# Chunk attention and a cosine router on one core: v and k loads in exchanged queues, and another order of the steps in the attention loop

## The chip, the cores and the metric

The kernel runs on one core of one Trainium2 chip. The metric is the device time of one execution in microseconds; before the change the median of three runs is 674.3 us (673.04 to 680.07). Engines: PE (TensorE, its matmuls; PEld are its weight loads), DVE (VectorE), ACT (ScalarE), POOL (GpSimd) and SP (SyncE, which only issues transfers). Transfers are issued from SP's queue or from POOL's.

## What is computed

Attention within chunks of 64 tokens, over 8 batches, 8 heads, 576 tokens and 64 channels per head; its output, 4608 tokens of 512 channels, goes through a router that gives each token to one of 8 experts, and through that expert's two layers. All of it is in float32.

```python
# q, k, v: (8, 8, 576, 64); chunk = 64, nc = 9
scores = scale * np.matmul(q_c, k_c.transpose(0, 1, 2, 4, 3))
scores = scores - np.max(scores, axis=-1, keepdims=True)
attn = np.exp(scores)
attn = attn / (np.sum(attn, axis=-1, keepdims=True) + 1e-09)
out = np.matmul(attn, v_c)
...
x = np.ascontiguousarray(attn_out.transpose(0, 2, 1, 3)).reshape(B * S, H * D)
...
xn = x / (np.linalg.norm(x, axis=-1, keepdims=True) + 1e-06)
logits = xn @ en.T / tau
expert_idx = np.argmax(logits, axis=1)
...
    h = np.maximum(x[mask] @ w1[e], 0.0)        # w1[e]: 512 x 1024
    out[mask] = gate_w[mask, None] * (h @ w2[e])  # w2[e]: 1024 x 512
```

## The kernel before

The kernel has two stages. The first is a loop over `t` from -3 to 38 in steps of one tile of 128 tokens (two chunks, all heads); there are `NT` = 36 tiles, 4.5 per batch. It computes the attention output of each tile, its squared norm and its logits, finds a place for each of its tokens among rows grouped by expert, and writes the token's row (2304 bytes: 512 channels, logits, token number, squared norm) to that place in a DRAM tensor `spots`. The second stage reads groups of 64 rows per expert from `spots`, multiplies them with the expert's weights and writes the results to the tokens' rows of the output. It is nearly all matmuls, and the diff does not touch it.

The schedule is manual: each engine runs its instructions in the order in which the program text issues them, and each queue its transfers. An instruction that has to wait for a buffer or an operand holds everything behind it on its engine. The steps of the loop work on different tiles at the same time:

- `load_qk(t)` loads a tile of k and of q, 256 KB each, as 1024 pieces of 256 bytes; a tile that spans two batches takes two transfers of each. There are four buffers of each, so a buffer is free again when `turn_qk` of four tiles before has read it. `load_v(b)` loads a batch's v, 8 transfers of one head (64 rows with 9 pieces of 256 bytes), into one of two buffers.
- `turn_qk(t)` transposes k and q on PE (128x128 float32 against the identity, four each); ACT copies k's out of PSUM, DVE q's.
- `scores(t)` runs 32 matmuls of 64x64; DVE takes the row maxima and subtracts them. There is one PSUM buffer for the scores, so the next tile's matmuls wait for this subtraction. `weights(t)` is the exp, in place, on ACT.
- `turn_a(t)` transposes the exp on PE, and ACT copies it out. `values(t)` runs 32 matmuls of 64x64 with v and a column of ones; DVE adds 1e-9 to the sums (the tile `rs`), takes the reciprocal and multiplies (L662) into a row buffer `xr`, of which there are eight. An iota on POOL writes the token numbers into the same row.
- `turn_x(t)` transposes that output on PE; ACT copies it out and takes the squares. Its operand is what L662 wrote.
- Every four tiles `logits` runs 32 matmuls of 128x32, `copy_logits` turns and copies the result, `pick` chooses the expert on DVE, and `place`, one tile later, counts ranks on PE and DVE. `put` then sends one tile's rows per tile with an indirect transfer on POOL, which is the scatter to `spots`.
- `constants()` fills small tables on POOL and a blank row block, all in tile 0; `clear_first()` writes the blank rows to nine blocks of `spots` from SP in tile 1. `load_early` (from tile 26, on SP) reads the first groups back, and `load_first` loads the first experts' weights, 4 MB in tile 28 and 4 MB in tile 30, from SP. `early_parts` are matmuls of the second stage that are put between the last tiles.

The transposes share three PSUM buffers (tag `tr`), in the order in which they are issued. Before the change the queues are these: k's first four tiles on SP and the others on POOL, q on POOL, v on SP.

Of the kernel before, what the change touches and what calls it, by code (L numbers as in the profile page):

```python
# [11 lines left out]
I32 = mybir.dt.int32  # L12
AF = mybir.ActivationFunctionType
ALU = mybir.AluOpType
# [4 lines left out]
P = 128  # L19
CH = 64  # L20
ROUND = 12582912.0
NO_ROW = 200000
# [3 lines left out]
def kernel(  # L26
# [11 lines left out]
    nc = tc.nc  # L38
    B, H, S, Dh = q.shape
    E, D = moe_expert_emb.shape  # L40
# [5 lines left out]
    NT = N // P  # L46
    NCB = S // CH
    G = P // 2
# [5 lines left out]
    NE = 4  # L54
# [20 lines left out]
    W = D + 64  # L75
# [94 lines left out]
    def first_rows(s, j, n):  # L170
        r0 = (0, E - 1)[s] * R + G * j
        return spots[r0 : r0 + G * n, :]
# [273 lines left out]
    with (  # L446
# [59 lines left out]
        in_g = one.tile([P, 1], FP32, name="in_g")  # L506
        e_p = one.tile([P, 1], FP32, name="e_p")

        def constants():
            nc.gpsimd.iota(io_i, pattern=[[1, NST]], base=0, channel_multiplier=0)  # L510
            nc.gpsimd.iota(part_i, pattern=[[0, 1]], base=0, channel_multiplier=1)
            make_upper_triangular(nc, sltb, val=1.0, diag=False)
            nc.gpsimd.memset(onesb, 1.0)
            nc.gpsimd.memset(blank, 0.0)
            nc.gpsimd.memset(blank[:, D + TOK : D + TOK + 1].bitcast(I32), NO_ROW)
            nc.gpsimd.memset(ones, 1.0)
            nc.gpsimd.memset(before, 0.0)
            nc.gpsimd.memset(eqb_all[:, 0], 0.0)
            nc.gpsimd.memset(jump[:, 1], 1.0)
            nc.gpsimd.memset(nb[:, 0:1], float((SPARE + R) // G))  # L520
            nc.gpsimd.tensor_copy(io, io_i)
            nc.gpsimd.tensor_copy(at, part_i)
            nc.gpsimd.tensor_scalar(pref, io[:, 0:E], -1.0, float(E), ALU.mult, ALU.add)
            nc.gpsimd.tensor_scalar(e_base, io[:, 0:E], float(R), None, ALU.mult)
            nc.gpsimd.tensor_scalar(second, at, float(G), None, ALU.is_ge)
            nc.gpsimd.tensor_scalar(is_0, at, 2.0, None, ALU.is_lt)
            nc.gpsimd.tensor_scalar(lim, at, -float(P), float(G * NE), ALU.mult, ALU.add)
            nc.gpsimd.tensor_scalar(step, second, -2.0, 1.0, ALU.mult, ALU.add)
            nc.gpsimd.tensor_scalar(first_s, second, -1.0, 1.0, ALU.mult, ALU.add)
            nc.gpsimd.tensor_scalar(back, io, -1.0, float(NST - 1), ALU.mult, ALU.add)  # L530
            nc.gpsimd.tensor_scalar(more_g, back, float(LEAST - NE), None, ALU.is_ge)
            nc.gpsimd.tensor_scalar(pair_g, back, float(LEAST - NE), None, ALU.is_equal)
            nc.gpsimd.tensor_tensor(more_g, more_g, pair_g, ALU.add)
            nc.gpsimd.tensor_tensor(pair_g, back, more_g, ALU.subtract)
            nc.gpsimd.memset(more_e[:, NSW - 1 : NSW], 1)
            nc.gpsimd.tensor_scalar(e_0, second, float(E - 1), None, ALU.mult)
            nc.gpsimd.tensor_scalar(e_1, e_0, 1.0, None, ALU.add)
            nc.gpsimd.tensor_scalar(ends_e, io[:, 0:E], 0.0, None, ALU.is_equal)
            nc.gpsimd.tensor_scalar(full, io[:, 0:E], float(E - 1), None, ALU.is_equal)
            nc.gpsimd.tensor_tensor(ends_e, ends_e, full, ALU.add)  # L540
            nc.gpsimd.tensor_scalar(done, ends_e, float(NE), None, ALU.mult)
            nc.gpsimd.tensor_scalar(ends_e, ends_e, is_0, None, ALU.mult)
            nc.gpsimd.tensor_scalar(in_g, second, -float(G), at, ALU.mult, ALU.add)
            nc.gpsimd.tensor_scalar(e_p, second, float(R), None, ALU.mult)
            nc.gpsimd.tensor_scalar(
                base_h, io[:, 0 : E // 2], 2.0 * R, e_p, ALU.mult, ALU.add
            )

        def clear_first():

            for s in range(2):
                nc.sync.dma_start(
                    out=first_rows(s, 0, NE).rearrange("(j p) w -> p j w", p=G),
                    in_=blank[0:G].unsqueeze(1).to_broadcast([G, NE, W]),
                )
            nc.sync.dma_start(out=spots[SPARE : SPARE + G, :], in_=blank[0:G])

        before = one.tile([P, E], BF16, name="before")
        qk_t, qkT, v_t, st = {}, {}, {}, {}

        def load_qk(t):

            for src, nm, eng in (
                (k, "kx", nc.sync if t < 4 else nc.gpsimd),
                (q, "qx", nc.gpsimd),
            ):
                x = qk_p.tile([P, H, Dh], FP32, tag=nm, name=nm)
                done = 0
                while done < P:
                    b, s = divmod(t * P + done, S)  # L570
                    n = min(P - done, S - s)
                    eng.dma_start(  # L572
                        out=x[done : done + n],
                        in_=src[b, :, s : s + n, :].rearrange("h p d -> p h d"),
                    )
                    done += n
                qk_t[nm, t] = x.rearrange("p h d -> p (h d)")

        def load_v(b, c0=0, c1=NCB, eng=nc.sync):

            t = v_sb[b % 2]
            for h in range(H):
                r0 = CH * (h % 2)
# [58 lines left out]
        def values(t):  # L642
# [3 lines left out]
            for i in range(NPAIR):  # L646
# [18 lines left out]
                rs.unsqueeze(3).to_broadcast([P, 2, NPAIR, Dh]),  # L665
                ALU.mult,
            )
            nc.gpsimd.iota(
                xr[:, t % NX, D + TOK : D + TOK + 1].bitcast(I32),
                pattern=[[0, 1]],  # L670
                base=P * t,
                channel_multiplier=1,
            )
            st[t] = {"x": x}

        def turn_x(t):
# [344 lines left out]

        early_t = 26
        ends = {sum(sizes[: b + 1]) - 1: b for b in range(len(sizes))}
        for t in range(-3, NT + 3):
# [202 lines left out]
```

## Time and profile before

One execution was profiled. It took 673.1 us; its span, from the first to the last instruction, is 671.3 us, with a mean granted TensorE clock of 0.983.

| engine | busy us of the span | in 73.13 to 88.42, a stretch of four tiles |
|---|---|---|
| PE | 623.0 | 14.52 |
| PE weight loads | 346.2 | 12.42 |
| DVE | 421.3 | 13.44 |
| ACT | 443.8 | 11.07 |
| POOL | 155.3 | 11.62 |

Row after row, the profile names line, engine, operation and tiles: `sc` are the scores in PSUM, `mx` their maxima, `a` what the exp works on, `pv` the values in PSUM, `xr` the row buffers, `tr` the transposes in PSUM. A timeline row gives the start and duration in microseconds, then, in brackets, how long the engine stood idle before it and what ended this. "issue" is idle time for which the profile shows no cause. The slices of the page are 16.8 us each. Waits are listed as total, number of times and longest one.

### The profile page before, as it was taken

Reading aid. Unit: us, or ns where it says so; the run is one execution under the profiler, and the core shown is the slowest. Engines: PE = TensorE matmul, PEld = TensorE weight load, DVE = VectorE, ACT = ScalarE, POOL = GpSimd, SP = SyncE. Lnnn points to the kernel's source line nnn. Section 1 sums busy time; section 2 is a strip of 40 time slices with the busy share of each in tenths; the row PEclk is TensorE's granted clock in tenths of the full one; section 3 lists DMA queues with packets and bytes.
Section 4 is the critical chain, followed back from the end, with each engine's and each line's share of the span. In section 5 each row is a group of like instructions: output and inputs, shape, how many; then the busy total and the mean of one; then the engine's idle time right before and its main releaser. Section 6 shows DMA issues by size and latency. Waiting matters only on the chain. (4 is left out here: it accounts for less than half of the span.)

```text
span 671.3 us, 24844 instructions
## 1 busy us (share of the span) xinstructions
PE 623.0 (93%) x9744; PEld 346.2 (52%) x9744; DVE 421.3 (63%) x1140; ACT 443.8 (66%) x776; POOL 155.3 (23%) x237
## 2 busy tenths in 40 slices
PE   6869998998898989999999999999999999999993
PEld 5658787885443446666434444334444444444431
DVE  4738888986598536547675566757655666565430
ACT  5627776775225847777777867778777677877740
POOL 8827787843310100010000100010001000100101
PEclk9969999999999989999999999999999999999997
DMA  9978999989818711113786111777811115411111
GB/s 256 275 180 233 275 288 269 275 246 371 330 55 300 285 45 35 50 34 111 290 305 210 50 42 43 290 274 253 327 52 50 38 47 167 166 43 34 50 31 35
DMA packets 94590, 112.66 MB, mean 168 GB/s; under 512 B 52364, under 2 KB 72588, under 8 KB 94456
## 3 DMA queue, kind: packets, MB, share of 16 engines
q1 hardware_dynamic: 82728, 72.84, 34.1%
q0 software_dynamic: 11696, 38.04, 17.0%
q8 instruction: 81, 1.33, 0.8%
q14 instruction: 53, 0.43, 0.2%
q10 hardware_dynamic: 32, 0.02, 0.0%
HBM read 334.71 MB, written 22.69 MB: 532 GB/s over the span
## 5 line engine op out<-in xcount | busy, mean ns | idle before, releaser
L413 PE MATMUL y_ps<-w,hT 128*32 128x512 f32 (+1 forms) x2368 | 273.2, 589 | 3.1 <-DVEq L299 3.1
L361 ACT ACTIVATE h<-C 64x256 f32<-64x256 f32 x264 | 178.6, 676 | 95.5 <-DVE C L374 68.9
L413 PEld LDWEIGHTS y_ps<-w,hT 128*32 128x32 f32 x2368 | 93.2, 110 | 153.6 <-issue 123.8
L428 POOL DMA_INDIRECT out_dram<-y,spot x36 | 34.9, 968 | 437.0 <-ACT C L377 198.0
L374 DVE TENSOR_TENSOR C<-C,h 128x256 f32<-128x256 f32 x231 | 96.1, 416 | 49.2 <-DVEq L299 42.5
L342 PE MATMUL h<-w,S 128*32 128x256 f32 x1056 | 98.1, 379 | 1.8 <-DVE w L291 1.8
L342 PE MATMUL h<-sums,xbT 128*32 128x256 f32 x1056 | 97.0, 379 | 0.0
L342 PE MATMUL h<-w,xbT 128*32 128x256 f32 x1056 | 79.4, 380 | 7.0 <-ACTq L299 5.8
L368 DVE STREAM_TRANSPOSE hT<-h 128x512 f32<-128x512 f32 x66 | 46.7, 708 | 44.1 <-ACT h L361 44.0
L342 PEld LDWEIGHTS h<-w,xbT 128*32 128x32 f32 x1056 | 40.8, 110 | 43.2 <-ACTq L299 13.5
L342 PEld LDWEIGHTS h<-w,S 128*32 128x32 f32 x1056 | 49.2, 110 | 24.4 <-DVE w L291 1.5
L342 PEld LDWEIGHTS h<-sums,xbT 128*32 128x32 f32 x1056 | 48.9, 110 | 21.9 <-ACT C L377 0.4
L227 DVE TENSOR_SCALAR rn<-rn 128x1 f32<-128x1 f32 x37 | 5.7, 153 | 72.1 <-ACT rn L224 72.1
L342 PE MATMUL h<-sums,S 128*32 128x256 f32 x528 | 48.7, 379 | 0.0
L800 POOL DMA_INDIRECT spots<-xr,dest x36 | 37.1, 1029 | 35.0 <-DVE dest L765 10.1
L203 DVE STREAM_TRANSPOSE xbT<-xin 128x256 f32<-128x256 f32 x73 | 44.4, 646 | 0.5 <-DVE hT L368 0.5
L224 ACT ACT_TABLE_LOAD x34 | 43.6, 1283 | 0.9 <-issue 0.4
L421 ACT ACTIVATE y<-y_ps,gate 128x512 f32<-128x512 f32 (+1 forms) x37 | 25.2, 682 | 28.6 <-issue 14.7
L231 ACT ACT_TABLE_LOAD x34 | 43.6, 1283 | 0.6
L682 ACT COPY xT<-tr 128x512 f32<-128x512 f32 x36 | 21.1, 586 | 34.2 <-PE tr L680 34.2
L651 PE MATMUL pv<-v,aT 64*64 64x65 f32 x1152 | 28.1, 226 | 9.0 <-DMA v<-in_v_dram 7.4
L572 POOL DMA_DIRECT2D kx<-in_k_dram x36 | 31.5, 876 | 16.4 <-PE tr L595 16.1
(202 smaller groups left out, 800.4 us busy)
## 6 DMA issues: line engine op xcount, KB each, us to landing
w<-in_moe_w_dram SPq DMA_DIRECT2D x74, 2048.0 KB
next_w<-in_moe_w_dram SPq DMA_DIRECT2D x67, 2048.0 KB
xin<-spots SPq DMA_DIRECT2D x158, 64.0 KB
qx<-in_q_dram POOLq DMA_DIRECT2D x32, 256.0 KB, 7.7
v<-in_v_dram SPq DMA_DIRECT2D x56, 144.0 KB
kx<-in_k_dram POOLq DMA_DIRECT2D x28, 256.0 KB, 5.7
spot<-spots SPq DMA_DIRECT2D x80, 4.0 KB
spots<-blank SPq DMA_DIRECT2D x2, 576.0 KB
```

What stands on the lines that cost most here:

```text
L203: nc.vector.transpose(xT[:, :, cols].rearrange("p c (b i) -> p b c i", i=Q), t[:, s * (D // 2) : (s + 1) * (D // 2)].rearrange("p (b i c) ...
L224: nc.scalar.activation(rn, spot[:, j % SPOTS, SQ : SQ + 1], AF.Sqrt)
L231: nc.scalar.activation(sh, sh, AF.Exp, accum_out=gate)
L342: nc.tensor.matmul(ps[t0 : t0 + Q], lhsT=a[:, c, s], rhs=w[:, r], start=c == 0, stop=c == KD // 2 - 1,)
L361: nc.scalar.activation(h[b][G * v : G * v + G, s].rearrange("p (k i) -> p k i", i=Q), x[G * s : G * s + G].rearrange("p (i k) -> p k i", i=Q),
L368: nc.vector.transpose(hT.rearrange("p k (s b i) -> p b s k i", b=2, i=Q)[:, b], h[b].rearrange("p s (k i) -> p s k i", i=Q),)
L374: nc.vector.tensor_tensor(out, a, b, op)
L413: nc.tensor.matmul(ps[Q * r : Q * r + Q, 0:w], lhsT=d["hT"][:, c, Q * t0 : Q * t0 + Q], rhs=w2_sb[s][buf_of(j)][:, c, d0 : d0 + w], start= ...
L428: ins = nc.gpsimd.indirect_dma_start(out=to, out_offset=bass.IndirectOffsetOnAxis(ap=at, axis=0), in_=y[:, 0:w], in_offset=None, bounds_ch ...
L572: eng.dma_start(out=x[done : done + n], in_=src[b, :, s : s + n, :].rearrange("h p d -> p h d"),)
L651: nc.tensor.matmul(pv[CH * c : CH * c + CH, par, i], lhsT=d["aT"][r0 : r0 + CH, i, CH * c : CH * c + CH], rhs=v_t[b][r0 : r0 + CH, i, cb, ...
L800: ins = nc.gpsimd.indirect_dma_start(out=spots, out_offset=bass.IndirectOffsetOnAxis(ap=at, axis=0), in_=m, in_offset=None, bounds_check=S ...
```

## The change

The diff does four things.

The order within a tile: it was a transposes (t), k and q transposes (t+3), logits, scores (t+2), logits' copy, place, x transposes (t-1), values (t), exp (t+2), pick. It becomes a transposes (t), logits, k and q transposes (t+3), exp (t+1), x transposes (t-1), scores (t+2), logits' copy, values (t), place, pick. All 128x128 transposes now stand together, and the two groups of 64x64 matmuls follow each other. The exp of a tile is issued one tile later, ahead of the x copy on ACT.

The queues: k is issued from SP for all tiles and v from POOL. Only the first four chunks of batch 0 stay on SP, and they come ahead of k and q of tiles 2 and 3. The rest of batch 0 goes out in tiles -2 and -1, four heads each. Batch b is issued in halves of four heads in two successive tiles, from the first tile with 2t // 9 + 1 = b: tiles 0 and 1 for batch 1, 5 and 6 for batch 2.

The constants become a generator, of which one piece per tile is issued from tile 0 on; the clearing writes become nine transfers of one block (64 rows), two per tile from tile 1 on.

The token numbers are written by one iota per four tiles, at the logits' copy, in place of one per tile.

```diff
-        def constants():
+        def constant_parts():
             nc.gpsimd.iota(io_i, pattern=[[1, NST]], base=0, channel_multiplier=0)
             nc.gpsimd.iota(part_i, pattern=[[0, 1]], base=0, channel_multiplier=1)
+            nc.gpsimd.memset(blank, 0.0)
+            nc.gpsimd.memset(blank[:, D + TOK : D + TOK + 1].bitcast(I32), NO_ROW)
+            yield
             make_upper_triangular(nc, sltb, val=1.0, diag=False)
             nc.gpsimd.memset(onesb, 1.0)
...
         def clear_first():
 
-            for s in range(2):
-                nc.sync.dma_start(
-                    out=first_rows(s, 0, NE).rearrange("(j p) w -> p j w", p=G),
-                    in_=blank[0:G].unsqueeze(1).to_broadcast([G, NE, W]),
-                )
+            for j in range(NE):
+                for s in range(2):
+                    nc.sync.dma_start(out=first_rows(s, j, 1), in_=blank[0:G])
+                    yield
             nc.sync.dma_start(out=spots[SPARE : SPARE + G, :], in_=blank[0:G])
...
-                (k, "kx", nc.sync if t < 4 else nc.gpsimd),
+                (k, "kx", nc.sync),
                 (q, "qx", nc.gpsimd),
...
-        def load_v(b, c0=0, c1=NCB, eng=nc.sync):
+        def load_v(b, c0=0, c1=NCB, heads=range(H), eng=nc.gpsimd):
 
             t = v_sb[b % 2]
-            for h in range(H):
+            for h in heads:
...
-            nc.gpsimd.iota(
-                xr[:, t % NX, D + TOK : D + TOK + 1].bitcast(I32),
-                pattern=[[0, 1]],
-                base=P * t,
-                channel_multiplier=1,
-            )
...
             nc.tensor.transpose(lt_ps, copied[b], ident)
+            nc.gpsimd.iota(
+                xr[:, t % NX : t % NX + n, D + TOK].bitcast(I32),
+                pattern=[[P, n]],
+                base=P * t,
+                channel_multiplier=1,
+            )
...
+        load_v(0, 0, 4, eng=nc.sync)
         load_qk(2)
         load_qk(3)
-        load_v(0, 0, 4)
-        load_v(0, 4, NCB)
...
             if 0 <= t < NT:
                 turn_a(t)
+            if t - 2 in ends:
+                logits(ends[t - 2])
             if t == early_t - 1:
                 count_early()
             if t + 3 < NT:
                 turn_qk(t + 3)
                 if t + 7 < NT:
                     load_qk(t + 7)
-            if t - 2 in ends:
-                logits(ends[t - 2])
-            if t == NT:
+            if t in (-2, -1):
+                load_v(0, 4, NCB, range(4 * (t + 2), 4 * (t + 2) + 4))
+            b = 2 * t // NCB + 1
+            if t >= 0 and b < B and v_half.get(b, 0) < 2:
+                m = v_half[b] = v_half.get(b, 0) + 1
+                load_v(b, heads=range(4 * m - 4, 4 * m))
+            if 0 <= t + 1 < NT:
+                weights(t + 1)
+            if 0 <= t - 1 < NT:
                 turn_x(t - 1)
             early_parts(t, 0)
             if 0 <= t + 2 < NT:
                 scores(t + 2)
             if t - 2 in ends:
                 copy_logits(ends[t - 2])
+            if 0 <= t < NT:
+                values(t)
             if t - 3 in ends:
                 place(ends[t - 3])
-            if 0 <= t - 1 < NT - 1:
-                turn_x(t - 1)
-            if 0 <= t < NT:
-                values(t)
-                b = (2 * t + 2) // NCB + 1
-                if b not in v_t and b < B and t > 1:
-                    load_v(b)
...
-            if 0 <= t + 2 < NT:
-                weights(t + 2)
             if t - 2 in ends:
                 pick(ends[t - 2])
...
-            if t == 0:
-                constants()
-            if t == 1:
-                clear_first()
+            if t >= 0:
+                next(constants, None)
+            if t >= 1:
+                next(clears, None)
+                next(clears, None)
```

More of the change, by code (lines that the diff above doesn't have):

```diff
@@ L507 @@
         e_p = one.tile([P, 1], FP32, name="e_p")
-        def constants():
+        def constant_parts():
             nc.gpsimd.iota(io_i, pattern=[[1, NST]], base=0, channel_multiplier=0)
             nc.gpsimd.iota(part_i, pattern=[[0, 1]], base=0, channel_multiplier=1)
+            nc.gpsimd.memset(blank, 0.0)
+            nc.gpsimd.memset(blank[:, D + TOK : D + TOK + 1].bitcast(I32), NO_ROW)
+            yield
             make_upper_triangular(nc, sltb, val=1.0, diag=False)
             nc.gpsimd.memset(onesb, 1.0)
-            nc.gpsimd.memset(blank, 0.0)
-            nc.gpsimd.memset(blank[:, D + TOK : D + TOK + 1].bitcast(I32), NO_ROW)
-            nc.gpsimd.memset(ones, 1.0)
+            nc.gpsimd.tensor_copy(io, io_i)
+            nc.gpsimd.tensor_copy(at, part_i)
+            yield
+            nc.gpsimd.tensor_scalar(pref, io[:, 0:E], -1.0, float(E), ALU.mult, ALU.add)
+            nc.gpsimd.tensor_scalar(e_base, io[:, 0:E], float(R), None, ALU.mult)
@@ L517, in constants @@
             nc.gpsimd.memset(before, 0.0)
             nc.gpsimd.memset(eqb_all[:, 0], 0.0)
+            nc.gpsimd.memset(ones, 1.0)
+            yield
             nc.gpsimd.memset(jump[:, 1], 1.0)
             nc.gpsimd.memset(nb[:, 0:1], float((SPARE + R) // G))
[L521 to L524, printed above, removed]
+            yield
@@ L525, in constants @@
             nc.gpsimd.tensor_scalar(second, at, float(G), None, ALU.is_ge)
             nc.gpsimd.tensor_scalar(is_0, at, 2.0, None, ALU.is_lt)
+            yield
             nc.gpsimd.tensor_scalar(lim, at, -float(P), float(G * NE), ALU.mult, ALU.add)
             nc.gpsimd.tensor_scalar(step, second, -2.0, 1.0, ALU.mult, ALU.add)
+            yield
             nc.gpsimd.tensor_scalar(first_s, second, -1.0, 1.0, ALU.mult, ALU.add)
             nc.gpsimd.tensor_scalar(back, io, -1.0, float(NST - 1), ALU.mult, ALU.add)
+            yield
@@ L531, in constants @@
             nc.gpsimd.tensor_scalar(more_g, back, float(LEAST - NE), None, ALU.is_ge)
             nc.gpsimd.tensor_scalar(pair_g, back, float(LEAST - NE), None, ALU.is_equal)
+            yield
             nc.gpsimd.tensor_tensor(more_g, more_g, pair_g, ALU.add)
             nc.gpsimd.tensor_tensor(pair_g, back, more_g, ALU.subtract)
+            yield
             nc.gpsimd.memset(more_e[:, NSW - 1 : NSW], 1)
             nc.gpsimd.tensor_scalar(e_0, second, float(E - 1), None, ALU.mult)
+            yield
@@ L537, in constants @@
             nc.gpsimd.tensor_scalar(e_1, e_0, 1.0, None, ALU.add)
             nc.gpsimd.tensor_scalar(ends_e, io[:, 0:E], 0.0, None, ALU.is_equal)
+            yield
             nc.gpsimd.tensor_scalar(full, io[:, 0:E], float(E - 1), None, ALU.is_equal)
             nc.gpsimd.tensor_tensor(ends_e, ends_e, full, ALU.add)
+            yield
             nc.gpsimd.tensor_scalar(done, ends_e, float(NE), None, ALU.mult)
             nc.gpsimd.tensor_scalar(ends_e, ends_e, is_0, None, ALU.mult)
+            yield
@@ L543, in constants @@
             nc.gpsimd.tensor_scalar(in_g, second, -float(G), at, ALU.mult, ALU.add)
             nc.gpsimd.tensor_scalar(e_p, second, float(R), None, ALU.mult)
+            yield
             nc.gpsimd.tensor_scalar(
@@ L549, in clear_first @@
         def clear_first():
-            for s in range(2):
-                nc.sync.dma_start(
-                    out=first_rows(s, 0, NE).rearrange("(j p) w -> p j w", p=G),
-                    in_=blank[0:G].unsqueeze(1).to_broadcast([G, NE, W]),
-                )
+            for j in range(NE):
+                for s in range(2):
+                    nc.sync.dma_start(out=first_rows(s, j, 1), in_=blank[0:G])
+                    yield
             nc.sync.dma_start(out=spots[SPARE : SPARE + G, :], in_=blank[0:G])
         before = one.tile([P, E], BF16, name="before")
-        qk_t, qkT, v_t, st = {}, {}, {}, {}
+        qk_t, qkT, v_t, st, v_half = {}, {}, {}, {}, {}
         def load_qk(t):
             for src, nm, eng in (
-                (k, "kx", nc.sync if t < 4 else nc.gpsimd),
+                (k, "kx", nc.sync),
                 (q, "qx", nc.gpsimd),
@@ L1023 @@
         ends = {sum(sizes[: b + 1]) - 1: b for b in range(len(sizes))}
+        constants, clears = constant_parts(), clear_first()
         for t in range(-3, NT + 3):
```

## The prediction

> **What bounds the kernel now.** I read the page's 40 slices first (16.8 us each), then the waits of 25 to 60 us, then a table of four-tile stretches, then the timeline of two tiles. From the 16th slice on PE stands at 9; that is the expert stage, which begins at about 190 us and which the diff does not touch. All of the change lies in the first 11 slices.
>
> ```profile
> PE   6869998998898989999999999999999999999993
> ...
> PEclk9969999999999989999999999999999999999997
> DMA  9978999989818711113786111777811115411111
> ```
>
> The third digit of PE and of PEclk is a 6. The waits of 25 to 60 us say why (us in total, times, longest):
>
> ```profile
> ACT aT L639 <- PE tr L637: 9.5, 1, 9.5
> ...
> DVE rs L659 <- PE pv L651: 9.2, 1, 9.2
> ...
> PE pv L651 <- DMA v<-in_v_dram: 7.3, 4, 5.6
> ```
>
> Everything waits once for the values of tile 4, and these for the second batch's v. Its loads start on SP at 21.50 us, behind the clearing writes (17.64 to 21.45), which waited for the constants on POOL. The starts of the a transposes are the kernel's pulse: tile 4 at 27.53, tile 5 at 40.37, tile 6 at 46.80. Undisturbed, a tile of tile 4's kind takes 3.30 us (24.23 to 27.53), and tile 5's, with logits, 4.41 (57.57 to 61.98 is the same kind), so the stall costs 9.54 + 2.02 = 11.6 us, the second part at a granted clock near half.
>
> After that nothing waits for a load. Four tiles, one round of logits, are the unit; columns are width, busy PE, PEld, DVE, ACT, POOL, clock, DMA share, GB/s:
>
> ```profile
> 57.57:73.13 15.56, 14.78 (x364) 12.53 (x359) 13.49 (x35) 11.07 (x27) 12.52 (x18) 1.00 1.03 296
> 73.13:88.42 15.29, 14.52 (x364) 12.42 (x358) 13.44 (x35) 11.07 (x27) 11.62 (x17) 1.00 0.99 274
> ```
>
> PE is 95% busy, DVE 88%; a clean round is 15.4 us. (The round from 103.72 took 16.79, with one 1.3 us gap of "issue" in it.) So a tile costs 3.86 us and PE's order sets it.
>
> **The change: the loop's order.** PE's order per tile was a, k and q transposes, scores(t+2), x transposes (t-1), values(t); now x comes before scores, and values last. It removes one of two turns from 128x128 to 64x64 per tile; each shows 0.17 us of PEld idle ("issue") ahead of the 64x64 loads, so 36 x 0.17 = 6.1 us if PE stays the bound. The page TensorEngine Tiling (Key Properties) of the Trainium skill has the same: a change of tiling mode drains TensorE; by it alone the loop would gain those 6.1 us.
>
> But the move closes a ring. The x transposes of t-1 read what DVE writes last for tile t-1, and scores(t+2) now stands behind them. Its legs, from the timeline:
>
> ```profile
> 75.60 0.56 PEld L611 LDWEIGHTS sc<-kxT,qxT 64*64 64x64 f32 x32 [0.20 <-DVE qxT L600]
> ...
> 76.36 0.69 DVE L619 TENSOR_REDUCE mx<-sc 128x8 f32<-128x512 f32 x1 [0.97 <-PE sc L611]
> ...
> 77.16 0.69 DVE L621 TENSOR_TENSOR a<-sc,mx 128x512 f32<-128x512 f32 x1
> ...
> 77.92 0.17 DVE L659 TENSOR_SCALAR rs<-pv 128x8 f32<-128x8 f32 x1
> ...
> 78.35 0.69 DVE L662 TENSOR_TENSOR xr<-pv,rs 128x512 f32<-128x512 f32 x1
> ```
>
> ```profile
> 83.91 0.42 PEld L680 LDWEIGHTS tr<-ident,xr 128*128 128x128 f32 x4 [0.49 <-issue]
> 83.94 0.63 PE L680 MATMUL tr<-ident,xr 128*128 128x128 f32 x4 [0.39 <-DVE xr L662]
> ...
> 84.50 0.56 PEld L651 LDWEIGHTS pv<-v,aT 64*64 64x64 f32 x32 [0.17 <-issue]
> ```
>
> Scores to maximum 0.76; maximum to subtraction 0.80; to rs 0.61 (27.25 to 27.86, a tile without the logits copy in between); rs to the product 0.43; the product 0.69; its end to the x transposes 0.12 (one that began at 83.10 ended at 83.79, and they loaded at 83.91); these to the next 64x64 loads 0.59. Sum 4.00 us. PE's own work in the meantime is 0.62 scores + 0.62 values + 0.39 + 0.44 + 0.44 transposes = 2.51, so it idles 0.9 us per tile; the q copy of 0.69 fits into DVE's 1.47 us of waiting. Before, values(t) alone stood behind x, and the slack hid it.
>
> In a round the logits (0.17 + 0.87 on PE) now fall into that idle time: 2.51 + 1.04 + 0.59 = 4.14, only 0.14 over. The logits' copy is in the ring: +0.16. The pick (0.97 on DVE after the product) with the q copy is 1.63 against 1.47: +0.16. Place is 0.8 early and about 1.2 late in the loop, with the q copy 1.5 to 1.9: +0.2. Round: 16.0 + 0.66 = 16.7 us against 15.4, +0.32 us per tile. PE is idle in pieces below 1 us: the gap of 1.3 us at 106.6 left the clock at 1.00, so I charge no clock.
>
> **The exp** moves from behind the squares of x to ahead of the x copy, for t+1. It is needed at the next tile's a transposes, 4.0 us after this tile's; a copy, k copy and exp take 0.66 + 0.1 + 0.57 + 0.57 + 0.62 = 2.5 us (about 3.6 with logits): hidden; the cover gone, it would add the rest of them. At the start it is not hidden: the first exp used to run at 12.03, its table load (1.28 us) at 8.74; now both stand behind the copy of the third k.
>
> **The loads.** k goes to SP for all tiles, v to POOL in halves of four DMAs, from tile 0 on for batch 1. At the start SP has k0, k1, eight v pieces, k2, k3. By 8 us SP's queue moved 4011 packets of 256 B, then 4370 in 8 to 20 us, 364 per us; k2 is its 5120th, so 11.1 us, against 10.8 when it was used before. With the k transposes and copy, then table load and exp (0.66 + 0.6 + 1.28 + 0.63), the first a transposes come at about 14.85 instead of 12.77: +2.1.
>
> Batch 1's v is now issued on POOL at tiles 0 and 1. POOL's issues before it are the q tiles at 0.9 us, eight v pieces, one constants piece; a v DMA of 576 rows of 256 B costs between the 0.68 of a half k tile (512) and the 0.89 of a whole one (1024), 0.7 taken. That puts its last issue near 25 us; loads landed in 5.7 to 7.7 us, so 31 to 33, and tile 4's values come at about 33.5. I take the stall as gone, with 1 us left for the start. If the cover fails, it costs what is late, up to 5 us.
>
> In the round POOL loses four k issues (3.6 us) and gains 7.1 v issues (5.0): 12.5 + 1.4 = 13.9 of 16.7 us. The token numbers, one iota per batch instead of per tile, take 0.5 us off and a wait for the scatters (11.7 us over the run, seven times). q loads and scatters queue behind a v half (2.8 us) twice per batch; q is four tiles ahead. On SP, k waits for its buffer and the clears stand behind it, two per tile (64 rows of 2304 B, 0.5 us each at the 0.91 MB in 3 us seen at 20.5 to 23.5). From tile 26, k33 to k35 queue behind the early row loads, which wait for scatters, about two tiles; they are four ahead. 1024 packets at 364 per us are 2.8 us, under 4.2.
>
> As to throughput, SP's 256 B packets took 17.5 ns of an engine alone (2460 packets, 95.9% of 16 engines in 40.6 to 43.4 us), POOL's loads 13.6 ns per 256 B (2.45 MB, 68.0% of 8 to 20 us). The exchange shifts only the first four k tiles' worth between them: 4096 x 4 ns / 16 = 1 us of engine time, charged at nothing. The page DMA: Bandwidth & Descriptors of the skill (Issuing engines are not separate DMA queues) speaks against a gain from it: DMAs of all issuers run on the same 16 engines and interleave, so the exchange by itself would be worth zero. The constants, 15.9 to 24.6 us on POOL in one piece, come in fourteen pieces under 1.2 us each beside POOL's slack; all are done by tile 14, and the first that a tile uses (pref, tile 5) by tile 2.
>
> **Sum.** First a transposes 14.85; tile 1 after 2.7 (no x yet, the exp decides); four rings to tile 5, 33.6; one round to tile 9, 50.3; 1 us for the start, 51.3; six rounds to tile 33, 151.5; 1.3 for the fetch gap seen once before, 152.8. Before: 151.57. So the stall's gain, 57.57 - 51.3 = 6.3, is given back over 24 tiles (24 x 0.32 = 7.6). The last two tiles keep the ring where PE waited before: +0.5. Expert weights issue sooner on SP, but no wait for them is there to go. Net +1.7 on the profiled run's 673.1 us (span 671.3): 674.8. The median, 674.3, lies 1.2 above that run, so 676.
>
> **Rivals.** (1) The ring does not bind, because its legs shrink once DVE is no longer full: PE stays the bound at 15.4 - 4 x 0.17 = 14.7 per round. Then 7 rounds give 14 us less than above, about 662. For it: every leg was taken on a full DVE. Against: four of them are dependent steps, back to back.
> (2) Slower: POOL's scatters come late behind the v halves, and DVE's product, which rewrites a row buffer eight tiles later, waits for the landing. By the rows (scatter landing 4.9 us, issue 1.05) the margin with 0.7 us per v DMA is about 0.9 us; it decides from 0.95 us per v DMA. At 1.4 us, 2 us are lost in most of the 7 batches, into the ring: +12, 688.
> (3) The change doesn't do what it says: batch 1's v is still late by 5 us or so: 681.
>
> **Chances.** Forecast 0.56, (1) 0.17, (2) 0.17, (3) 0.10. The forecast's own range is 670 to 682 (ring 3.9 to 4.1, start 0 to 4). Leaving out half of (1) and half of (2), 664 to 688. Within 1% (6.7 us, about what can be told here) is 0.52: most of the forecast and half of (3); faster 0.19, (1) and a little; slower 0.29, (2), half of (3) and the forecast's upper end.
>
> **What would show it.** Right: a transposes 4.0 us apart, rounds of 16.5 to 16.9, and the row of x transposes waiting for DVE's product, some 0.9 us in most tiles; no 9 us wait at tile 4; clock 1.00 in the third slice. Wrong: rounds under 15.5, or DVE waiting for scatters, or PE for k or v.

## The result, and the profile after

The changed kernel takes 687.1 us (median of four runs, 685.1 to 687.7); beside it the kernel before takes 676.0 (four runs, 673.0 to 680.1). The ratio is 1.0149, with a 95% interval of 1.0102 to 1.0195: slower by one and a half per cent. The prediction was 676, between 664 and 688. The profiled execution took 685.1 us; its span is 683.3, against 671.3.

The page's slices first (17.1 us each), for PE, its granted clock and the DMA share:

```profile
PE   5789878787898999999999999999999999999990
...
PEclk9999999999999999999999999999999999999996
DMA  9988888898727811112786111777811116311111
```

The 6 in the third slice is gone, in PE and in the clock. In its place PE shows 7 and 8 from the fifth to the eleventh slice, where it had 8 and 9. The waits of the first 180 us (total, times, longest) name what took over:

```profile
ACT aT L652 <- PE tr L650: 32.4, 36, 3.6
...
DVE xr L675 <- DMA spots<-xr,dest: 8.5, 6, 2.0
PE tr L687 <- DVE lmax L737: 7.5, 8, 2.2
PE tr L687 <- DVE w L775: 5.6, 7, 1.6
PE tr L687 <- ACT a L644: 5.6, 7, 0.8
```

L687 are the x transposes. They wait in most tiles; the instructions that the rows name (`lmax`, `w`, the exp) are those that end near that time, while the operand is DVE's product at L675. That product itself waits six times for a scatter (`spots`) to land, which it never did before. No row says that values wait for v.

The a transposes are the pulse again. Cut there, and at the end of the last matmul, the two profiled spans differ like this:

| stretch | before, us | after, us | difference |
|---|---|---|---|
| start to tile 0 | 12.77 | 15.40 | +2.63 |
| tile 0 to 9 | 44.80 | 35.91 | -8.89 |
| tile 9 to 30 | 82.94 | 91.64 | +8.70 |
| tile 30 to 35 | 20.27 | 28.25 | +7.98 |
| tile 35 to the last matmul's end | 499.58 | 496.51 | -3.07 |
| last matmul's end to the span's end | 10.96 | 15.63 | +4.67 |
| span | 671.32 | 683.34 | +12.02 |

The -3.07 means little: in the fourteen profiles of this study that stretch lies between 496.5 and 501.8, whatever the kernel.

**The ring**, in the changed kernel's timeline (start, duration, engine, line, operation; in brackets the idle time before):

```profile
79.82 0.56 PEld L624 LDWEIGHTS sc<-kxT,qxT 64*64 64x64 f32 x32 [0.17 <-issue]
...
80.58 0.69 DVE L632 TENSOR_REDUCE mx<-sc 128x8 f32<-128x512 f32 x1
...
81.38 0.69 DVE L634 TENSOR_TENSOR a<-sc,mx 128x512 f32<-128x512 f32 x1
...
81.99 0.15 DVE L672 TENSOR_SCALAR rs<-pv 128x8 f32<-128x8 f32 x1
...
82.42 0.69 DVE L675 TENSOR_TENSOR xr<-pv,rs 128x512 f32<-128x512 f32 x1
...
83.22 0.42 PEld L687 LDWEIGHTS tr<-ident,xr 128*128 128x128 f32 x4 [1.02 <-ACT a L644]
...
83.81 0.56 PEld L624 LDWEIGHTS sc<-kxT,qxT 64*64 64x64 f32 x32 [0.17 <-issue]
```

From scores to scores: 0.76, 0.80, 0.61, 0.43, 0.69, 0.11 and 0.59 us, 3.99 in all; the sum in the prediction was 4.00. PE's share of the idle time lies ahead of the x transposes: 0.8 to 1.0 us before their weight loads, 0.6 to 0.8 before their matmuls. A clean round, here from a second profile of the same kernel (width, busy PE, PEld, DVE, ACT, POOL, clock, DMA share, GB/s), is 16.18 us:

```profile
53.72:69.90 16.18, 14.23 (x364) 12.10 (x359) 13.41 (x35) 11.49 (x26) 14.91 (x24) 1.00 0.88 256
```

Its tiles are 4.56, 3.81, 3.82 and 3.99 us. Most rounds are not clean: in the first profile the six from tile 9 on take 16.18, 17.41, 17.92, 16.83, 18.48 and 21.02.

**The scatters.** One such wait, in the changed kernel's timeline:

```profile
135.71 3.00 POOL L597 DMA_DIRECT2D v<-in_v_dram  x4
139.01 1.05 POOL L813 DMA_INDIRECT spots<-xr,dest  x1 [0.30 <-issue]
...
140.96 3.00 POOL L597 DMA_DIRECT2D v<-in_v_dram  x4
...
145.85 0.69 DVE L675 TENSOR_TENSOR xr<-pv,rs 128x512 f32<-128x512 f32 x1 [2.01 <-DMA spots<-xr,dest]
...
146.69 1.04 PE L687 MATMUL tr<-ident,xr 128*128 128x128 f32 x4 [2.21 <-DVE lmax L737]
```

The scatter of tile 21 goes out as soon as four v transfers are through. Its row buffer is wanted again by the product of tile 29, which waits 2.01 us until 145.85, 6.8 us after that scatter's issue; PE waits with it. In the kernel before, no wait of DVE stood there; the iota on POOL met the same landing (11.7 us in all), and only POOL stood still for it. These waits also tell how long a scatter took before the change. The longest, the scatter of tile 25 and the iota of tile 33, which writes the same row buffer:

```profile
147.83 0.99 POOL L800 DMA_INDIRECT spots<-xr,dest  x1 [0.46 <-POOL xr L668]
...
155.32 0.12 POOL L668 IOTA xr<- 128x1 int32 x1 [2.83 <-DMA spots<-xr,dest]
```

That is 7.5 us from issue to release. Of the seven such waits one ends 4.5 us after its scatter's issue and six end after 6.2 to 7.5. The median landing of 4.9 us on the page of the kernel before rests on the 6 of 36 scatters whose landing the profile tells (5.9 at most). In the changed kernel the six waits of DVE end 4.8 to 7.4 us after the issue. So a scatter was about as slow before; there DVE's product for tile 33 came at 155.86, half a microsecond after the landing, and in six tiles of the changed kernel the product comes to the row first.

**The end of the loop**, five tiles in one row each (columns as above), before and after:

```profile
140.51:160.78 20.27, 17.50 (x435) 14.05 (x428) 18.24 (x52) 13.47 (x32) 6.39 (x11) 1.00 0.87 307
```

```profile
142.95:171.20 28.25, 20.84 (x432) 15.89 (x428) 18.68 (x52) 13.33 (x29) 7.72 (x11) 0.88 0.88 306
```

The same PE work takes 20.84 us instead of 17.50, because the clock is 0.88, and 4.6 us more are idle. The clock is not low throughout: it stands at 0.50 for 3.41 us from 146.76 and again for 3.41 us from 167.24, and at 1.00 between. The 2.21 us gap above comes just before the first fall: the four x transposes after it take 1.04 us instead of 0.63. No gap over 0.8 us stands in the 3.4 us before the second, but PE was busy for only 1.93 of them (1.20 of the 3.41 us before the first).

**The close.** POOL's last row in each timeline:

```profile
663.59 0.98 POOL L428 DMA_INDIRECT out_dram<-y,at  x1 [4.66 <-ACTq L1181]
```

```profile
671.04 0.97 POOL L428 DMA_INDIRECT out_dram<-y,at  x1 [4.75 <-ACTq L1196]
```

From its end to the span's end 6.7 us pass before and 11.3 after, with no work of the program in them.

### The profile page after: what moved, and what is told of

Its sections match the earlier page's. It is cut to its first block, busy times and chain, and to the rows that moved or that the text cites. A ratio compares the mean times of both kernels' runs of the same rounds, so it can differ in the third digit from the quotient of the medians.

```text
span 683.3 us, 24845 instructions
## 1 busy us (share of the span) xinstructions
PE 620.1 (91%) x9744; PEld 334.6 (49%) x9744; DVE 421.8 (62%) x1140; ACT 447.6 (66%) x776; POOL 170.1 (25%) x238
## 3 DMA queue, kind: packets, MB, share of 16 engines
q0 software_dynamic: 13040, 38.57, 17.1%
## 5 line engine op out<-in xcount | busy, mean ns | idle before, releaser
L413 PEld LDWEIGHTS y_ps<-w,hT 128*32 128x32 f32 x2368 | 87.6, 110 | 158.2 <-issue 145.5
L342 PE MATMUL h<-w,S 128*32 128x256 f32 x1056 | 101.0, 380 | 1.8 <-DVE w L291 1.8
L342 PE MATMUL h<-sums,xbT 128*32 128x256 f32 x1056 | 100.8, 383 | 0.0
L597 POOL DMA_DIRECT2D v<-in_v_dram x64 | 47.2, 770 | 0.0
L687 PE MATMUL tr<-ident,xr 128*128 128x128 f32 x144 | 22.9, 282 | 22.5 <-DVE lmax L737 7.5
L652 ACT COPY aT<-tr 128x512 f32<-128x512 f32 x36 | 21.1, 586 | 32.4 <-PE tr L650 32.4
```

The source lines that it names most:

```text
L342: nc.tensor.matmul(ps[t0 : t0 + Q], lhsT=a[:, c, s], rhs=w[:, r], start=c == 0, stop=c == KD // 2 - 1,)
L413: nc.tensor.matmul(ps[Q * r : Q * r + Q, 0:w], lhsT=d["hT"][:, c, Q * t0 : Q * t0 + Q], rhs=w2_sb[s][buf_of(j)][:, c, d0 : d0 + w], start= ...
L597: eng.dma_start(out=t[r0 : r0 + CH, h // 2, c0:c1, 0:Dh], in_=v[b, h].rearrange("(c k) d -> k c d", k=CH)[:, c0:c1],)
```

## The experiments

In the edits, "new loads" are the change's loads, clears and constants. Ratios are to the kernel before, timed on the same chip; its median was 686.4 us on the first group's chip, 675.7 and 675.8 on the others, so only ratios are compared across groups. A ratio is an estimate over all runs, and differs from the quotient of the two medians by up to 0.2%; differences in microseconds are those of medians.

### First group: the ring and the queues

**The kernel before with the new order alone** (its loads, clears, constants and iotas kept):

```diff
+            if t - 2 in ends:
+                logits(ends[t - 2])
...
-            if t - 2 in ends:
-                logits(ends[t - 2])
-            if t == NT:
+            if 0 <= t + 1 < NT:
+                weights(t + 1)
+            if 0 <= t - 1 < NT:
                 turn_x(t - 1)
             early_parts(t, 0)
...
-            if t - 3 in ends:
-                place(ends[t - 3])
-            if 0 <= t - 1 < NT - 1:
-                turn_x(t - 1)
             if 0 <= t < NT:
                 values(t)
...
+            if t - 3 in ends:
+                place(ends[t - 3])
...
-            if 0 <= t + 2 < NT:
-                weights(t + 2)
```

> The kernel before with the new order within a tile alone; all loads, constants, clears and token numbers as before. Ring theory (x transposes ahead of scores make a 4.0 us ring): the 10 us wait for v at tile 4 stays, plain tiles are 4.0 us apart in place of 3.3, rounds 16.5 to 16.9 in place of 15.4, so 8 to 11 us slower than before: about 685. No wait of DVE's product for scatters. Rival (the exchanged queues cost it all, the order is free or saves its 6 us): 668 to 677.

692.6 us, ratio 1.0073 [1.0040, 1.0105]. The stall stays (tile 4 to 5: 12.87 us), plain ring tiles take 3.99, and DVE waits for a scatter once, 0.2 us. The order costs by itself, though less than expected: 6.2 us by the medians and 0.7% by the ratio, where 8 to 11 us stood. And with none of the new loads, tiles 30 to 35 already take 27.65 us, at a clock of 0.88. The kernel before has no profile on this chip; in the one of the result it took 20.27.

**The change with the x transposes back behind scores:**

```diff
-            if 0 <= t - 1 < NT:
+            if t == NT:
                 turn_x(t - 1)
...
                 copy_logits(ends[t - 2])
+            if 0 <= t - 1 < NT - 1:
+                turn_x(t - 1)
```

> The changed kernel with the x transposes put back behind the scores and the logits' copy, ahead of values; loads, exp and the rest as changed. Ring theory: plain tiles back to 3.3 us, tile 9 at 46 to 48 in place of 51.3. Scatter theory (v halves on POOL hold up the scatters, and DVE's product waits for their landing): a faster loop leaves them less time, so the waits of DVE for scatters stay or grow over the 8.5 us of the changed kernel; rounds 15.6 to 17. Both together: 674 to 681. If the order is free: 685 to 689.

686.9 us, ratio 1.0001 [0.9969, 1.0034], where the change has 1.0149 (on another chip). Plain tiles are 3.30 us again, tile 9 comes at 51.44 and not at 46 to 48, but DVE now waits 13.4 us for scatters, seven times, against 8.5. A quicker loop comes to the row buffers earlier, and these are not free sooner.

**The change with k on POOL from tile 4 on and v on SP, at the change's tiles:**

```diff
-                (k, "kx", nc.sync),
+                (k, "kx", nc.sync if t < 4 else nc.gpsimd),
...
-        def load_v(b, c0=0, c1=NCB, heads=range(H), eng=nc.gpsimd):
+        def load_v(b, c0=0, c1=NCB, heads=range(H), eng=nc.sync):
```

> The changed kernel with k back on POOL (from tile 4 on) and v on SP, still in early halves; order as changed. Scatter theory: the 8.5 us of DVE waiting for scatters go, and with them the slow stretch from tile 30 on; rounds 16.2 to 16.8 up to tile 33, so 8 to 12 us faster than the changed kernel: 675 to 679. Plain tiles stay at 4.0 us (ring). Rival (k on SP or the queue's rate is of no account, only the ring costs): 685 to 688.

690.2 us, ratio 1.0067 [1.0033, 1.0101]; by the ratios some 5 to 6 us better than the change, where 8 to 12 were expected. Plain ring tiles are 3.99, and no wait of DVE for scatters is left: in this order they go when v leaves POOL. The slow end of the loop stays (tiles 30 to 35: 28.08 us).

**Both edits together:**

> Both of the two edits: x behind the scores, and k on POOL, v on SP in early halves. If ring and scatters are the two costs and the stall at tile 4 is what the change gained, all three are right here: tile 9 at 46 to 48, rounds 15.3 to 15.7, tile 33 at 139 to 142, 10 us faster than the kernel before: 662 to 668. If the stall comes back with v on SP: 674 to 678.

679.2 us, ratio 0.9896 [0.9858, 0.9934]; faster than both kernels, though not for all the reasons expected. Tile 9 comes at 52.26, not at 46 to 48 (the first a transposes start only at 19.33), the rounds vary between 15.05 and 18.65, and DVE waits 5.0 us for scatters, in four times, with v on SP. So v on POOL is not the only cause of these waits: with the same loads the slower loop of the run before had none. The end of the loop is shorter (tiles 30 to 35: 23.05 us). One line of its windows shows a plain tile in which PE does not idle:

```profile
33.91:37.21 3.30, 3.30 (x87) 2.83 (x81) 3.01 (x7) 2.81 (x8) 1.97 (x5) 1.00 0.94 285
```

Against the run before it, on the same chip and with the same loads, the place of the x transposes is worth 690.2 - 679.2 = 11.0 us.

### Second group: the order and the loads, one without the other

**The change again**, as a control on this chip:

> The changed kernel itself, on the chip of the runs of this call, so that they have one base. 1.010 to 1.020 times the kernel before, as first measured. If the ratio depends on the chip, it lies outside of this.

687.1 us, ratio 1.0155 [1.0095, 1.0214].

**The change with place ahead of values**, as before the change:

```diff
+            if t - 3 in ends:
+                place(ends[t - 3])
             if 0 <= t < NT:
                 values(t)
-            if t - 3 in ends:
-                place(ends[t - 3])
```

> The changed kernel with place ahead of values, as it was before. Late-place theory: behind values and DVE's product the batch's first destination is ready some 2 us later, the scatters of a batch start that much later, and DVE's product waits for their landing (8.5 us in the changed kernel); with place first these waits fall below 3 us, and the time falls by 3 to 6 us. Against it, place's 0.8 to 1.2 us of DVE now lie in the ring of 4.0 us once per round, 7 to 9 us in all, of which 0.2 us per round was paid anyway. Late-place theory: 4 us faster to 2 us slower than the changed kernel. V-on-POOL theory (the v halves alone make the scatters late): the waits stay at 6 us or more, and the time rises by 4 to 8 us.

685.6 us, ratio 1.0144 [1.0093, 1.0195], the same as the control. Yet the waits differ:

```profile
DVE xr L675 <- DMA spots<-xr,dest: 0.8, 1, 0.8
```

The control has 6.8 us there. With place early, the places are known sooner and the scatters are in time; but place's matmuls and DVE's work then lengthen the ring, whose clean round becomes 4.57 + 4.04 + 4.42 + 4.01 = 17.0 us. The slower ring itself gives a scatter more time, some 1.7 us over eight tiles; how much of the fall from 6.8 to 0.8 us is that, and how much the earlier place, this run does not part. Seven rounds at 0.8 us are 5.7 us, about the 6.0 that the waits for scatters lost. Two loops bind the stage by turns: the ring, and the row buffers' loop (product, logits, pick, place, scatter, landing, the product eight tiles later).

**The new loads under the whole old order** (exp of t+2 last, x transposes behind scores, place ahead of them):

> The changed kernel with the whole order within a tile as before (exp of t+2 last, place and x between scores and values): only loads, constants, clears and token numbers are new. Order theory: first a transposes at 12.8 to 13.5 us in place of 15.4, no stall at tile 4, plain tiles 3.3 us apart, and 8 to 12 us faster than the kernel before (ratio 0.982 to 0.988). If v on POOL makes the scatters late whatever the order: waits of DVE for scatters of 5 us or more, ratio 0.990 to 1.000.

677.8 us, ratio 1.0037 [1.0001, 1.0073]. On this chip the order costs 687.1 - 677.8 = 9.2 us. But the new loads alone gain nothing either, where 8 to 12 us were expected: DVE waits 9.9 us for scatters, up to 3.3, although place is early here. Tile 9 comes at 49.86 us, 7.7 ahead of the kernel before; tiles 9 to 30 then lose 4.3, tiles 30 to 35 lose 8.1 (28.34 us, against 27.83 with the change's order on this chip) and the close 4.7.

**The same with k on POOL and v on SP:**

> As the run before it, with k back on POOL and v on SP in early halves: what is new is when v, constants and clears are issued. If the exchange of queues is worth nothing by itself: within 3 us of the run before it. V-on-POOL theory: 4 to 8 us faster than it, with waits of DVE for scatters under 2 us; ratio to the kernel before 0.975 to 0.985.

676.1 us, ratio 1.0003 [0.9970, 1.0035]. Against the run before it that is 1.7 us, within the 3 that stood for an exchange worth nothing; the waits of DVE for scatters fell to 2.4 us. Here the stall is gone and nothing of the change's order is left, and still nothing is won. Its stretches: tile 9 at 51.38 us, 6.2 ahead of the kernel before; tile 30 still 6.4 ahead; tile 35 at 162.62, 1.8 behind. Tiles 30 to 35 take 28.5 us instead of 20.3, and the timeline says why:

```profile
133.07 3.67 SPq L153 DMA_DIRECT2D xin<-spots  x2
...
139.92 3.45 SPq L597 DMA_DIRECT2D v<-in_v_dram  x4
143.42 1.26 SPq L128 DMA_DIRECT2D w<-in_moe_w_dram  x2
...
143.99 0.33 PE L664 MATMUL pv<-v,aT 64*64 64x65 f32 x4 [2.21 <-DMA v<-in_v_dram]
...
147.84 0.48 PE L664 MATMUL pv<-v,aT 64*64 64x65 f32 x2 [1.23 <-DMA v<-in_v_dram]
```

The second half of the last batch's v stands on SP behind the early row reads, which wait for scatters. Tile 31's values stop four times; that tile takes 10.35 us, and the clock is 0.79 in 138 to 154 us.

### Third group: the last batch's v

**The last run's loads, but the last batch's v from POOL**, under the old order:

```diff
-                load_v(b, heads=range(4 * m - 4, 4 * m))
+                load_v(b, heads=range(4 * m - 4, 4 * m), eng=nc.gpsimd if b == B - 1 else nc.sync)
```

> The new loads and constants under the old order, with k on POOL and v on SP as in the older run of this kind, but the last batch's v from POOL, so that it does not stand behind the early row loads on SP. Theory A (the stall at tile 4 is worth its 6 us, and in the older run tile 31's late v, 10.35 us instead of 3.8 and a granted clock near half after it, took them back): tiles 31 and 32 within 5 us of each other, tile 33's a transposes near 145 to 147 us, ratio to the kernel before 0.986 to 0.992. Rival B (the gain is eaten elsewhere, by scatters or a later start): ratio 0.997 to 1.003, with DVE waits for scatters of 5 us or more.

680.7 us, ratio 1.0073 [1.0040, 1.0106]: outside both. Tile 9 is at 51.42 and tile 30 at 135.05, 5.5 us ahead of the kernel before; then tile 31 takes 10.56 us and the five tiles 30.7. No wait for v is left. Freed of v, SP issues the first experts' weights (4 MB) at 134.24, ahead of two scatters that stand behind v on POOL:

```profile
134.24 1.40 SPq L128 DMA_DIRECT2D w<-in_moe_w_dram  x2
134.34 2.97 POOL L597 DMA_DIRECT2D v<-in_v_dram  x4
137.63 1.06 POOL L813 DMA_INDIRECT spots<-xr,dest  x1 [0.32 <-issue]
...
139.04 1.04 POOL L813 DMA_INDIRECT spots<-xr,dest  x1 [0.17 <-issue]
...
149.17 0.69 DVE L675 TENSOR_TENSOR xr<-pv,rs 128x512 f32<-128x512 f32 x1 [6.10 <-DMA spots<-xr,dest]
```

The scatter of 137.63 is that of tile 22, and the product of tile 30 has its row at 149.17, after 11.5 us. In the kernel before the same load went out at 147.12, and the scatter of 147.83, 0.7 us behind it, took the 7.5 us shown above; but there no v transfers from POOL stood just ahead of it. In the changed kernel, with v ahead and no weights yet, the scatter of 139.01 took 6.8. So the 11.5 us were seen with weights and v together.

**The same loads with the change's order:**

> The change with the same loads as the run before it in this group (k on POOL, v on SP, last batch's v from POOL): the ring without v's bursts on POOL. Theory A (ring and late scatters are two separate prices): DVE waits for scatters under 1 us, clean rounds of 16.2 to 16.7 us, seven rounds at 0.9 to 1.3 us above the old order's, so 6 to 9 us above the run with the old order, ratio 0.996 to 1.005, against 1.015 for the change. Rival B (the ring is the whole price): ratio 1.012 to 1.018 as the change.

691.2 us, ratio 1.0235 [1.0197, 1.0273], above both ranges. Up to 125 us DVE waits 1.3 us for scatters; all the rest of its 10.7 us lies in the last tiles, as above (weights at 142.08, the scatter of tile 22 at 146.6, the row free at 157.8).

**The same loads and order, x transposes behind scores:**

> The same loads, the change's order with the x transposes put back behind scores: place still after values, exp one tile ahead. Theory A (only the x transposes' place closes the ring): plain tiles 3.30 us, ratio within 0.4% of the run with the whole old order of this group, 0.986 to 0.994; place after values shows as DVE waits for scatters of 2 to 6 us. Rival B (place and exp have prices of their own): 0.5% or more above the run with the old order.

682.8 us, ratio 1.0124 [1.0071, 1.0177]. By the medians 0.3% above the run with the old order, by the ratios 0.5%, and the intervals overlap: the time does not decide between the bounds of 0.4 and 0.5%. But its scatter waits are 16.5 us and not 2 to 6, and tiles 9 to 30 take 87.9 us against 83.6. In these two profiles place and exp, later and earlier in the tile, so cost 4.3 us there. (The two profiled runs are 4.2 us apart, the medians 2.2.) The x transposes' place is worth 691.2 - 682.8 = 8.4 us here.

**The change with v in three parts** (three, three and two heads in successive tiles):

```diff
-            if t >= 0 and b < B and v_half.get(b, 0) < 2:
+            if t >= 0 and b < B and v_half.get(b, 0) < 3:
                 m = v_half[b] = v_half.get(b, 0) + 1
-                load_v(b, heads=range(4 * m - 4, 4 * m))
+                load_v(b, heads=range(3 * m - 3, min(3 * m, H)))
```

> The change with each batch's v issued as 3, 3 and 2 heads in three successive tiles instead of 4 and 4 in two. Theory A (a scatter is late because it stands behind a burst of four v issues, 3.0 us): DVE's waits for scatters fall from 8.5 us to under 4, time 3 to 5 us below the change, ratio 1.007 to 1.011. Rival B (POOL's sum of work makes them late): waits of 6 to 10 us, ratio 1.012 to 1.018. A wait for v at tiles 9, 13, 18 would show that the third part comes too late.

682.6 us, ratio 1.0107 [1.0064, 1.0150]. The time is what the burst theory expected, the 7.0 us of waits for scatters are what the other did, and the interval overlaps the change's. Whether the burst or the sum of POOL's work makes scatters late stays open.

### The close, over all profiles

POOL's last two long instructions in each trace (a semaphore step of its queue, then a drain), with the transfers it had issued apart from the indirect ones:

```
                                          transfers  step    drain   last matmul's end to span's end
v on SP (before, and four runs)               76     0.63   1.93-1.94    10.8 to 11.8 us
last batch's v on POOL (three runs)           84     1.26     4.55       13.4 to 14.4
all v on POOL (the change, and four runs)    104     1.44     5.28       15.6 to 16.0
all v on POOL, in three parts (one run)      104     1.48     5.45       15.0
```

Order and chip make no difference to the drain; v on POOL does. The 4.67 us of the first table are 3.35 of drain, 0.81 of the step and 0.5 of other. The drain is not in proportion to the count (8 more transfers: 2.6 us, 20 further ones: 0.7), and what the drain waits for was not tried.

## Why the prediction was right and wrong

**The stall.** Right: no wait for v at tile 4, and tile 9 came at 51.31 us where 51.3 was worked out. That it agrees so closely is luck: the second profile of the same kernel has it at 53.72. First a transposes at 15.40, for 14.85.

**The ring.** Right in mechanism and size per tile: 3.99 for 4.00, leg by leg. The round was over-sized: 16.18 clean for 16.7; that the logits' copy and the pick fitted into DVE's waits is the likely reason, not tested. On equal loads the x transposes' place costs 8.4 and 11.0 us, so rival (1), a ring that does not bind, falls. The Trainium skill's page TensorEngine Tiling (Array Packing), Key Properties, says that a change of tiling mode drains TensorE. Of these gaps, for which the prediction worked out 6.1 us, one of 0.17 us per tile did go (the 64x64 loads of values follow those of scores with none), but a PE that idles 0.8 us per tile gains nothing by it.

**The scatters.** Here a step failed: the margin of "about 0.9 us" with 0.7 us per v transfer, by which rival (2) was to decide at 0.95. The transfers took 0.77 us and DVE already waited 8.5 us in six times. The term that was mis-sized is the landing, put at 4.9 us: that is the median of the six scatters whose landing the profile of before tells. The seven waits of the iota, which the prediction counts only as time that POOL saves, show 6.2 to 7.5 us for six others, so the 0.9 us were not there. The margin had also left out that place, now behind values, makes the scatters later; with place ahead of values, and a slower ring, 0.8 us of the wait is left. Rival (2) was right in kind, at a lower threshold; its +12 us, so near to what was measured, is luck, for most of the miss lies in the last tiles and the close. DVE waiting for scatters was one of the signs of being wrong that the prediction names.

**The last tiles.** The largest mis-sized term: "the last two tiles +0.5", and "Expert weights issue sooner on SP, but no wait for them is there to go". By the prediction's rates tile 30 would have come at 141.0 and tile 35 at 162.5, 21.5 us later; it took 28.25. The new loads bring this loss under the old order too (28.34 us): what comes sooner on SP (early reads, weights) meets v and the scatters in the same 16 us. Three kernels show three forms of it: v behind the early reads (k on POOL, v on SP), scatters behind v (the change), scatters behind v and beside the weights (the last batch's v from POOL). But loads are not the whole of it: the new order with the old loads took 27.65 us there, with 0.2 us of waits for scatters, on the slower chip. Each half of the change can lose some 7 us in these tiles, and together they lose no more; what shares they have is open. The same page that was held against a gain from the exchange, DMA: Bandwidth & Descriptors (Issuing engines are not separate DMA queues), says that transfers of all issuers run on the same 16 engines and interleave. The third form is in line with it (11.5 us for a scatter on POOL with 4 MB from SP in flight), but v stood ahead of that scatter too.

**The clock.** "So I charge no clock" failed as well: the two stretches at half clock make 20.84 - 17.50 = 3.3 us of the loss in tiles 30 to 35. The gap of 1.3 us from which the term was put at nothing was a single one; here pieces of idle time of 0.7 to 2.2 us came together.

**The exchange.** Charged at about nothing. Under the old order it costs 677.8 - 676.1 = 1.7 us with overlapping intervals; in it are 4.1 us more of closing (15.69 against 11.58), less what the last batch's v saves.

**The close.** Not in the prediction at all: +4.67 us.

Summed from tile 9 on, the prediction missed about 1.9 us up to tile 30, 6.7 in tiles 30 to 35 and 4.7 at the close, and had 3.1 too many in the expert stage: 10.2 of the 10.3 us from 674.8 to 685.1. The direction was given 0.29. The forecast's own range, 670 to 682, does not hold the measured 687.1; the stated one, to 688, does because half of rival (2) was let in. The forecast "gain and ring cancel" was near for the ring and the stall; what the sum lacked was the end of the loop and of the program.

**Open.** The fastest version (x transposes behind scores, k on POOL, v on SP, ratio 0.9896) ran on one chip only; why that chip takes 1.6% longer for the kernel before was not looked into. Twelve row buffers, which would part the scatters from the product, were not tried.

## What to carry to other kernels

Where an edit makes a step wait for another engine's result and puts the next start behind it, add up the legs of that ring from the timeline and compare with the period: here that was right to 0.01 us. Before a landing time goes into a margin, see how many transfers it was read from, and look at what already waits for it. A stall that is removed sends all later transfers out earlier, so the place to look next is where several queues meet with no slack, here the end of the stage; in one run 6.4 us won early were all lost in five tiles. A transfer had a price at three places here: its issue, its landing beside what else moves, and the close of the queue that issued it.

## What the hardware showed

- POOL's drain at the end of the program grows from 1.93 to 5.28 us when v is issued there in halves, to within 0.01 us in five profiles each.
- In the kernel before, a scatter of one tile's rows landed in 4.1 to 5.9 us (the six whose landing the profile tells), and six others that an iota waited for in 6.2 to 7.5. One took 11.5 us with four v transfers just ahead of it on its queue and 4 MB of weights issued 3.4 us ahead on the other.
- In the changed kernel a PE gap of 2.21 us that ends at 146.69 us is followed by half clock for 3.41 us; one of 2.23 us that ends at 93.23 is not. At 167.24 the clock falls for as long with no gap over 0.8 us in the 3.4 us before it, of which PE was idle for 1.5 in all.
- The kernel before takes 686.4 us (30 runs) on one chip, 675.7 and 675.8 on two others.
